# The inverse 47-point step of a spectral layer with FFN: segments of 8 n1, cosine and sine rows in one product, one copy out

## The chip, the cores and the metric

The kernel runs on one core of a Trainium2 chip. The metric is the device time of one execution in microseconds, the median of several runs; the trace comes from one further execution that was profiled.

## The reference

```python
X = np.fft.rfft(x, axis=1)                      # x: 8 x 3008 x 256
Yr = Xr @ w_r - Xi @ w_i + b_r                  # D = 256 mixed at each frequency
Yi = Xr @ w_i + Xi @ w_r + b_i
Y = shrunk(Yr) + 1j * shrunk(Yi)                # sign(a) * max(|a| - 0.01, 0)
y = np.fft.irfft(Y, n=3008, axis=1)
...
h = y @ w_in                                    # 24064 tokens x 2048
g = h * np.clip(h + 3, 0, 6) / 6
out = g @ w_out                                 # 24064 x 256
```

## The kernel before

The transform over 3008 = 64 x 47 positions is done in two steps with matrices, over n1 (64) and n2 (47). Since the input is real, 24 of the 47 frequencies k2 suffice. For each of 8 batches `stage1` makes the 47-point transforms of the input and stores them in DRAM (`scr1`), `middle` does the 64-point transforms, the mixing with `w_r` and `w_i` and the shrinking, and the 64-point transforms back, and stores the result in DRAM (`scr2`: cosine or sine part, n1, k2, D). `segment(b, k)` does the last step, the sum over k2 for each n2, and writes y into `raw`, transposed: 128 partitions hold half of D (`dh` is the half), and the free axis holds positions, cut in chunks of T = 512 (`raw[c]`, two buffers).

A segment of before takes 10 n1 (the seventh of a batch takes 4). Its data `qt` comes with two loads, one for the cosine part and one for the sine part, each with 5 n1 x 24 k2 = 120 rows in 2 groups. For each half of D four products (cosine and sine, two groups; L847) give the even part and the odd part for 24 n2 each, 240 columns a part. ScalarE copies the odd part out of PSUM into `odd` (L857). VectorE adds both for n2 = 0 to 23 (`direct`, L862) and subtracts them for the mirrored n2 (`mirrored`, L876), into `raw`, cut where a chunk ends or where a run of 23 is broken. So the positions within a segment do not stand in natural order; the host puts them right at the end. The products are in full fp32, for which the trace shows two records, with a weight load each, for one matmul of the program.

`prepare(c)` takes `raw[c]` once it is whole: GpSimd forms four differences (L924), ScalarE rounds seven blocks (L130), and GpSimd makes the remainders (L131); the results are `yb`. The FFN runs over 47 chunks x 8 = 376 units (c, f). A unit multiplies `yb` by blocks of `w_in` in a Strassen scheme of seven products (`pb`, `ps_a`, all at L137); ScalarE copies the partial sums `p`, `u` and `h` (L946, L978), VectorE adds (L949), ScalarE applies the first part of the gate (`r`, L1001) and rounds (`gs`, L1006), VectorE does the rest (L1003, L1007), and the products with `w_out` add up in `po` (`down`).

The order is written out by hand. In the loop over units each unit has four places (`fill`), and `slots` says which step of which generator goes to which place: `begin[b, k]` is the unit in which a segment starts, at least 8.5 units ahead of the chunk in which it begins and 3 ahead of the next segment; `lay` spreads a segment's three steps (load, first half of D, second half) over three units. The first two segments of batch 0 and the third are laid by themselves, at the start. All loads and stores are issued on SyncE's queue, in program order. `ps_a` has four PSUM buffers, `qt` one, `raw` two.

Of the kernel before, what the change touches and what calls it, by code (L numbers as in the profile page):

```python
# [9 lines left out]
F32 = mybir.dt.float32  # L10
# [4 lines left out]
ALU = mybir.AluOpType  # L15
# [6 lines left out]
B, S, D, FF = 8, 3008, 256, 2048  # L22
N1, N2 = 64, 47
NK = N2 // 2 + 1
LAM = 0.01
P = 128

J = 5
SEGS = tuple((n1, min(2 * J, N1 - n1)) for n1 in range(0, N1, 2 * J))
R47 = J * NK  # L30
NFT = FF // P

T = 512
# [4 lines left out]
def sequence():  # L38

    n1, n2 = np.meshgrid(np.arange(N1), np.arange(N2), indexing="ij")  # L40
    return (N2 * n1 + N1 * n2) % S


def positions():

    pos, order = sequence(), []
    for first, n in SEGS:
        n1 = first + np.arange(n)
        order += [pos[n1, :NK].reshape(-1), pos[n1][:, N2 - np.arange(1, NK)].reshape(-1)]
    return np.concatenate(order)  # L50


def constants():

    n1, n2 = np.arange(N1), np.arange(N2)
    k1, k2 = np.arange(N1), np.arange(NK)
    freq = np.zeros((N1, NK), np.int64)
    for k in range(S):
        if k % N2 < NK:
            freq[k % N1, k % N2] = k  # L60
    sign = np.where(freq <= S // 2, 1.0, -1.0)
    t47 = 2 * np.pi * np.outer(k2, k2) / N2
    t64 = 2 * np.pi * np.outer(n1, k1) / N1
    c47, s47, c64, s64 = np.cos(t47), np.sin(t47), np.cos(t64), np.sin(t64)


    f47 = np.zeros((J, NK, 2, J, NK))
    for j in range(J):
        f47[j, :, 0, j] = c47
        f47[j, :, 1, j] = s47  # L70

    f64 = np.zeros((2, N1, NK, 2, N1))
    f64[0, :, :, 0] = c64[:, None]
    f64[1, :, :, 0] = -s64[:, None]
    f64[0, :, :, 1] = -s64[:, None] * sign.T[None]
    f64[1, :, :, 1] = -c64[:, None] * sign.T[None]

    g64 = np.zeros((2, N1, 2, N1))
    g64[0, :, 0] = c64.T
    g64[1, :, 0] = -s64.T  # L80
    g64[0, :, 1] = -s64.T
    g64[1, :, 1] = -c64.T
    g64 *= 2.0 / S

    sgn = np.ones((2, N1, 2, NK // 2))
    sgn[:, :, 1] = sign.reshape(N1, NK // 2, 2).transpose(2, 0, 1)
    sgn[0, N1 // 2 + 1 :, :, 0] = 0.0
    for k in (0, N1 // 2):
        sgn[0, k, 0, 0] = 0.5
        sgn[0, k, 1, 0] = 0.0  # L90
    f = lambda a, *s: np.ascontiguousarray(a.reshape(*s).astype(np.float32))
    return {
        "f47": f(f47, R47, 2 * R47),
        "f64": f(f64, P, NK * P),
        "g64": f(g64, P, P),
        "g64u": f(np.broadcast_to(g64.transpose(1, 0, 2, 3)[None], (2, N1, 2, 2, N1)), P, 2 * P),
        "sgn": f(sgn, P, NK),
    }


@with_exitstack
def spectral_ffn(ctx: ExitStack, tc: tile.TileContext, x, w_r, w_i, bias, w_in, w_out, f47, f64, g64, g64u, sgn, out):
    nc = tc.nc
    const = ctx.enter_context(tc.tile_pool(name="const", bufs=1))
    sb = ctx.enter_context(tc.tile_pool(name="sb", bufs=1))
# [8 lines left out]
    def space(shape, dt, name, tag=None):  # L114
        tag = tag or name
        return sb.tile(shape, dt, name=name, tag=tag, bufs=depth.get(tag, 1))
# [187 lines left out]

    f47_s = [const.tile([R47, 2 * R47], dt, name="f47_" + t) for t, dt in (("hi", F32R), ("lo", F32R), ("all", F32))]
    nc.sync.dma_start(out=f47_s[2], in_=f47)
    scr1, scr2 = {}, {}

    def rows_of(b, n1, w):
# [389 lines left out]
    band()  # L699
    band()  # L700
    nc.sync.dma_start(out=g64u_s, in_=g64u)
    nc.sync.dma_start(out=bias_s[P // 2 :], in_=bias[P // 2 :])
    warm(8)
    split(*w_re)
# [112 lines left out]
    raw = {}  # L817

    def segment(b, k):
        n1, n = SEGS[k]  # L820
        gr = 2 if n == 2 * J else 1
        rows = n // gr * NK
        w = n * NK
        t0 = b * S + n1 * N2
        begins = b == 0 and k < 2
        qt = space([P, 2, 2, D], F32, "qt", "r" if begins else "xin" if (b, k) == (0, 2) else "qt")
        for cs in range(2):
            src = scr2[b][cs, n1 : n1 + n].rearrange("(g j) k d -> (j k) g d", g=gr)
            nc.sync.dma_start(out=qt[:rows, cs, :gr], in_=src)
        for c in range(t0 // T, (t0 + n * N2 - 1) // T + 1):  # L830
            if c not in raw:
                raw[c] = space([P, 2, T], F32, "raw")
        yield

        def places(at, size):

            done = 0
            while done < size:
                c, q = divmod(t0 + at + done, T)
                m = min(size - done, T - q)  # L840
                yield c, q, at + done, at + done + m
                done += m

        def products(ps, dh, groups):
            for cs in range(2):
                for g in groups:
                    nc.tensor.matmul(  # L847
                        out=ps[:, cs * w + g * rows : cs * w + (g + 1) * rows],
                        lhsT=qt[:rows, cs, g, dh * P : (dh + 1) * P],
                        rhs=f47_s[2][:rows, cs * R47 : cs * R47 + rows],  # L850
                        start=True,
                        stop=True,
                    )

        def odd_part(ps, n):
            odd = space([P, 2 * R47], F32, "odd", "p1" if begins else "xi")[:, :n]
            nc.scalar.copy(out=odd, in_=ps[:, w : w + n])  # L857
            return odd

        def direct(ps, odd, dh, lo, hi):  # L860
            for c, q, lo, hi in places(lo, hi - lo):
                nc.vector.tensor_tensor(out=raw[c][:, dh, q : q + hi - lo], in0=ps[:, lo:hi], in1=odd[:, lo:hi], op=ALU.add)  # L862

        def mirrored(ps, odd, dh):
            some = lambda a: a.rearrange("p (n q) -> p n q", q=NK)[:, :, 1:]
            m = NK - 1
            for c, q, lo, hi in places(w, n * m):
                lo, hi = lo - w, hi - w
                while lo < hi:
                    row, col = divmod(lo, m)  # L870
                    if col == 0 and hi - lo >= m:
                        r1, c1 = hi // m, m
                    else:
                        r1, c1 = row + 1, min(m, col + hi - lo)
                    size = (r1 - row) * (c1 - col)
                    nc.vector.tensor_tensor(  # L876
                        out=raw[c][:, dh, q : q + size].rearrange("p (n q) -> p n q", n=r1 - row),
                        in0=some(ps[:, :w])[:, row:r1, col:c1],
                        in1=some(odd)[:, row:r1, col:c1],
                        op=ALU.subtract,  # L880
                    )
                    lo, q = lo + size, q + size

        if (b, k) == (0, 1):
            lead = T - t0
            pss = [room(), room()]
            for dh in range(2):
                products(pss[dh], dh, range(1))
            for dh in range(2):
                direct(pss[dh], odd_part(pss[dh], lead), dh, 0, lead)  # L890
            yield
            for dh in range(2):
                products(pss[dh], dh, range(1, gr))
                odd = odd_part(pss[dh], w)
                direct(pss[dh], odd, dh, lead, w)
                mirrored(pss[dh], odd, dh)
                yield
            return
        for dh in range(2):
            ps = room()  # L900
            products(ps, dh, range(gr))
            odd = odd_part(ps, w)
            direct(ps, odd, dh, 0, w)
            mirrored(ps, odd, dh)
            yield


# [198 lines left out]
    per = S / 64  # L1106
    begin = {}
    for b in reversed(range(B)):
        for k in reversed(range(len(SEGS))):
            first = 8 * ((b * S + SEGS[k][0] * N2) // T)  # L1110
            begin[b, k] = min([first - 8.5, *([begin[b, k + 1] - 3] if (b, k + 1) in begin else [])])
            if k + 1 == len(SEGS) and (b + 1, 0) in begin:
                begin[b, k] = min(begin[b, k], begin[b + 1, 0] - 3)
    for c in range(1, NC):
        g = prepare(c)
# [9 lines left out]
        slots.setdefault(q, []).append(g)  # L1125
    lay(g, 15, 7.5, 12.5)
    for b in range(B):
        for k in range(len(SEGS)):
            if (b, k) not in ((0, 0), (0, 1)):
                if (b, k) == (0, 2):  # L1130
                    lay(segment(b, k), 3, 1, 2.5)
                else:
                    lay(segment(b, k), 3, max(0, begin[b, k]), max(3, begin[b, k] + 3))
        if b:
            pairs(middle(b), max(13, per * (b - 1) - 14), begin[b, 0] - 1.5)
        if b > 1:
            lay(stage1(b), 16, max(14, per * (b - 2) - 10), per * (b - 1) - 16)
# [93 lines left out]
```

## Time and profile before

| | |
|---|---|
| median of 3 runs | 2578.67 us (2576.99 to 2579.1) |
| the profiled execution | 2579.09 us |
| its span, first to last instruction | 2577.3 us |
| granted TensorE clock | 1.000 of full speed |

Of the profiled execution's time all but 1.8 us lies in the span. An engine's share of busy time is over the whole span; "x" is a count of instructions. Matmuls overlap and their ends are modelled, so the distance from one start to a later one tells more than a duration. In groups of instructions, the numbers behind the bar are the busy time in us and the mean of one instruction in ns, and behind the second bar the idle time of the engine ahead of them and what ended it. Of the stages: up to 98 us the first transforms run; from 98 us the FFN's units run, the first of them beside what is left of the weights' preparation; from 140 us on they run steadily, and the transforms of the next batches are laid between them.

### The profile page before, as it was taken

The numbers are of one execution on the slowest core, as the hardware profiler recorded it, in microseconds if no ns is written. First come the engines' busy times: TensorE is split into PE (matmuls) and PEld (weight loads), VectorE is DVE, ScalarE is ACT, GpSimd is POOL, SyncE is SP. The second block draws the span as 40 slices with busy tenths as digits, with TensorE's granted clock in tenths as the row PEclk, the third lists the DMA queues.
The fourth block names the chain that finished last, engine by engine and source line by source line (L and its number), as shares of the span: only waits on it lengthen the run. The fifth ranks groups of instructions, "written<-read, shape, count | busy, mean of one in ns | idle before, by whom it ended". The sixth has DMA issues, their size and how long they took to land.

```text
span 2577.3 us, 45562 instructions
## 1 busy us (share of the span) xinstructions
PE 2558.3 (99%) x16502; PEld 2290.4 (89%) x16502; DVE 1952.9 (76%) x3169; ACT 1965.1 (76%) x4330; POOL 741.5 (29%) x722
## 2 busy tenths in 40 slices
PE   9999999999999999999999999999999999999999
PEld 6788889899999989988899888999999999999998
DVE  6978877777777877777777777777777777766676
ACT  5777777777777777777777777777777777777877
POOL 2233422343133421433313432133411221121210
PEclk9999999999999999999999999999999999999999
DMA  8534422232122221222212322222321121110000
GB/s 279 173 93 133 131 73 69 83 95 73 57 79 82 88 83 49 83 83 80 81 55 77 91 87 67 64 77 84 91 62 53 56 73 49 37 32 25 20 17 17
DMA packets 147209, 199.65 MB, mean 77 GB/s; under 512 B 16303, under 2 KB 101927, under 8 KB 146983
## 3 DMA queue, kind: packets, MB, share of 16 engines
q1 hardware_dynamic: 146983, 196.73, 25.2%
q8 instruction: 130, 2.13, 0.3%
q14 instruction: 96, 0.79, 0.1%
HBM read 99.68 MB, written 74.97 MB: 68 GB/s over the span
## 4 chain that ended last, share of the span: by engine, by line
PE 90%; DVE 4%; ACT 3%; DMA 2%; issue 1%; POOL 0%; SPq 0%; DVEq 0%; ACTq 0%; POOLq 0%
PE po L137 38%; PE ps_a L137 25%; PE pb L137 19%; PE ps_a L847 3%; PE ps_a L737 3%; PE ps_a L459 1%; DVE r L1003 1%; DVE gs L1007 1%; ACT gs L1006 1%; DVE h L949 1%; DMA xin<-in_x 0%; ACT r L1001 0%; PE ps_a L494 0%; PE pb L426 0%; DMA scr<-a 0%
## 5 line engine op out<-in xcount | busy, mean ns | idle before, releaser
L137 PE MATMUL po<-gs,w_out_hi 128*128 128x512 f32 x3008 | 948.4, 396 | 1.5 <-DVE gs L1007 1.4
L1001 ACT ACTIVATE r<-h,three 128x512 f32<-128x512 f32 x750 | 541.7, 725 | 149.7 <-DVE h L949 135.1
L1003 DVE SCALAR_TENSOR_TENSOR r<-r,h 128x1024 f32<-128x1024 f32 x375 | 491.1, 1309 | 212.0 <-ACT r L1001 210.9
L137 PEld LDWEIGHTS po<-gs,w_out_hi 128*128 128x128 f32 x3008 | 565.1, 188 | 87.4 <-DVE gs L1007 3.9
L137 PE MATMUL po<-gs,w_out_lo 128*128 128x512 f32 x1504 | 611.3, 406 | 0.2 <-ACT gs L1006 0.2
L1007 DVE TENSOR_TENSOR gs<-r,gs 128x1024 fp32r<-128x1024 f32 x375 | 479.4, 1278 | 163.9 <-ACT gs L1006 163.4
L137 PE MATMUL pb<-yb,w_in_hi 128*128 128x256 f32 x3008 | 564.6, 280 | 0.0
L1006 ACT CAST gs<-r 128x512 fp32r<-128x512 f32 x750 | 429.1, 620 | 175.1 <-DVE r L1003 172.0
L137 PEld LDWEIGHTS pb<-yb,w_in_hi 128*128 128x128 f32 x3008 | 460.9, 188 | 33.3
L131 POOL TENSOR_TENSOR yb<-T,yb 128x256 fp32r<-128x256 f32 x184 | 193.0, 1051 | 840.2 <-ACT yb L130 840.1
L137 PE MATMUL ps_a<-yb,w_in_hi 128*128 128x256 f32 x2256 | 432.6, 280 | 0.1
L137 PE MATMUL pb<-yb,w_in_lo 128*128 128x256 f32 x1504 | 423.7, 282 | 3.9 <-ACT p L946 2.0
L949 DVE TENSOR_TENSOR h<-ps_a,u 128x256 f32<-128x256 f32 x752 | 313.8, 417 | 133.2 <-PE ps_a L137 129.7
L137 PEld LDWEIGHTS ps_a<-yb,w_in_hi 128*128 128x128 f32 x2256 | 345.4, 188 | 17.2 <-DVE yb L131 0.3
L946 ACT COPY u<-pb 128x256 f32<-128x256 f32 x752 | 279.3, 372 | 104.1 <-PE pb L137 102.4
L137 PE MATMUL ps_a<-yb,w_in_lo 128*128 128x256 f32 x1128 | 318.2, 282 | 3.0 <-DVE h L949 2.5
L137 PEld LDWEIGHTS pb<-yb,w_in_lo 128*128 128x128 f32 x1504 | 283.3, 188 | 42.0 <-ACT p L946 3.5
L137 PEld LDWEIGHTS po<-gs,w_out_lo 128*128 128x128 f32 x1504 | 283.5, 188 | 20.4 <-issue 2.4
L137 PEld LDWEIGHTS ps_a<-yb,w_in_lo 128*128 128x128 f32 x1128 | 212.0, 188 | 25.6 <-DVE h L949 8.6
L946 ACT COPY p<-pb 128x256 f32<-128x256 f32 x376 | 138.7, 369 | 38.2 <-PE pb L137 36.4
L949 DVE TENSOR_TENSOR h<-ps_a,p 128x256 f32<-128x256 f32 x376 | 156.4, 416 | 3.2 <-ACT p L946 2.6
L131 POOL TENSOR_TENSOR xs<-xin,xs 120x512 fp32r<-120x512 f32 (+1 forms) x42 | 55.2, 1314 | 310.7 <-ACT xs L130 288.5
(165 smaller groups left out, 3456.1 us busy)
## 6 DMA issues: line engine op xcount, KB each, us to landing
xin<-in_x SPq DMA_DIRECT2D x48, 512.0 KB, 3.6
bt<-scr SPq DMA_DIRECT2D x96, 256.0 KB, 3.1
scr<-pt SPq DMA_DIRECT2D x96, 256.0 KB, 2.0
out<-ot SPq DMA_DIRECT2D x93, 256.0 KB, 2.0
scr<-a SPq DMA_DIRECT2D x96, 240.0 KB, 2.5
qt<-scr SPq DMA_DIRECT2D x96, 240.0 KB, 3.5
zt<-tc SPq DMA_DIRECT2D x336, 64.0 KB, 2.0
f<-in_f SPq DMA_DIRECT2D x96, 128.0 KB, 2.8
```

The costliest lines, as they stand in the source:

```text
L131: (on or nc.vector).tensor_tensor(out=lo, in0=src, in1=hi.bitcast(F32), op=ALU.subtract)
L137: nc.tensor.matmul(out=ps, lhsT=a, rhs=b, start=start and n == 0, stop=stop and n == len(todo) - 1, skip_group_check=more,)
L459: nc.tensor.matmul(out=to, lhsT=x[:, xh, dh, which], rhs=w_s[w][wh][:, dh * D : (dh + 1) * D], start=False, stop=n == 2 and (which, dh) == ...
L737: nc.tensor.matmul(out=psv[:, dh, :, u, :], lhsT=data[:, u, dh * P : (dh + 1) * P], rhs=f[:, u, :], start=True, stop=True,)
L847: nc.tensor.matmul(out=ps[:, cs * w + g * rows : cs * w + (g + 1) * rows], lhsT=qt[:rows, cs, g, dh * P : (dh + 1) * P], rhs=f47_s[2][:row ...
L946: nc.scalar.copy(out=t, in_=ps)
L949: nc.vector.tensor_tensor(out=hs[i][:, u, half * H : (half + 1) * H], in0=ps, in1=keep.pop((i, n)), op=ALU.add)
L1001: nc.scalar.activation(out=r[:, u], in_=h[:, u], func=AF.Relu, bias=three, scale=1.0)
L1003: nc.vector.scalar_tensor_tensor(out=r, in0=r, scalar=6.0, in1=h, op0=ALU.min, op1=ALU.mult)
L1006: nc.scalar.copy(out=t[:, 0, u], in_=r[:, u])
L1007: nc.vector.tensor_tensor(out=t[:, 1], in0=r, in1=t[:, 0].bitcast(F32), op=ALU.subtract)
```

## The change

A segment takes 8 n1, eight to a batch. `qt` now has 96 rows (2 n1 x 24 k2 of cosine, and below them as many of sine) in 4 groups of two n1. A new constant `i47` of 96 rows and 2 x 47 = 94 columns holds cosine and sine for all 47 n2, so that one product gives two n1 in full, in natural order. For each half of D there are four products of 96 rows and 94 columns, beside each other in one PSUM tile of 376 columns. One copy per half moves the result into `raw`, cut where a chunk ends: ScalarE moves the first half of D, VectorE the second. `odd`, `direct`, `mirrored` and `places` go. The slots are laid for eight segments. `positions` becomes natural order.

```diff
+PARTS = tuple(range(0, N1, 8))
...
+    turn = 2 * np.pi * np.outer(k2, n2) / N2
+    i47 = np.zeros((2, 2, NK, 2, N2))
+    for j in range(2):
+        i47[0, j, :, j] = np.cos(turn)
+        i47[1, j, :, j] = np.sin(turn)
...
+    i47_s = const.tile([4 * NK, 2 * N2], F32, name="i47")
...
     nc.sync.dma_start(out=g64u_s, in_=g64u)
+    nc.sync.dma_start(out=i47_s, in_=i47)
     nc.sync.dma_start(out=bias_s[P // 2 :], in_=bias[P // 2 :])
...
     def segment(b, k):
-        n1, n = SEGS[k]
-        gr = 2 if n == 2 * J else 1
-        rows = n // gr * NK
-        w = n * NK
-        t0 = b * S + n1 * N2
+        n1, w = PARTS[k], 2 * N2
+        rows = 2 * NK
+        t0, size = b * S + n1 * N2, 4 * w
...
-        qt = space([P, 2, 2, D], F32, "qt", "r" if begins else "xin" if (b, k) == (0, 2) else "qt")
+        qt = space([P, 4, D], F32, "qt", "r" if begins else "xin" if (b, k) == (0, 2) else "qt")
         for cs in range(2):
-            src = scr2[b][cs, n1 : n1 + n].rearrange("(g j) k d -> (j k) g d", g=gr)
-            nc.sync.dma_start(out=qt[:rows, cs, :gr], in_=src)
+            src = scr2[b][cs, n1 : n1 + 8].rearrange("(g j) k d -> (j k) g d", g=4)
+            nc.sync.dma_start(out=qt[cs * rows : (cs + 1) * rows], in_=src)
...
         def products(ps, dh, groups):
-            for cs in range(2):
-                for g in groups:
-                    nc.tensor.matmul(
-                        out=ps[:, cs * w + g * rows : cs * w + (g + 1) * rows],
-                        lhsT=qt[:rows, cs, g, dh * P : (dh + 1) * P],
-                        rhs=f47_s[2][:rows, cs * R47 : cs * R47 + rows],
-                        start=True,
-                        stop=True,
-                    )
...
+            for g in groups:
+                nc.tensor.matmul(
+                    out=ps[:, g * w : (g + 1) * w],
+                    lhsT=qt[: 2 * rows, g, dh * P : (dh + 1) * P],
+                    rhs=i47_s,
+                    start=True,
+                    stop=True,
+                )
+
+        def moved(ps, dh, lo, hi):
+            while lo < hi:
+                c, q = divmod(t0 + lo, T)
+                m = min(hi - lo, T - q)
+                to, of = raw[c][:, dh, q : q + m], ps[:, lo : lo + m]
+                if dh:
+                    nc.vector.tensor_copy(out=to, in_=of)
+                else:
+                    nc.scalar.copy(out=to, in_=of)
+                lo += m
...
         for dh in range(2):
             ps = room()
-            products(ps, dh, range(gr))
-            odd = odd_part(ps, w)
-            direct(ps, odd, dh, 0, w)
-            mirrored(ps, odd, dh)
+            products(ps, dh, range(4))
+            moved(ps, dh, 0, size)
             yield
...
-        for k in reversed(range(len(SEGS))):
-            first = 8 * ((b * S + SEGS[k][0] * N2) // T)
+        for k in reversed(range(len(PARTS))):
+            first = 8 * ((b * S + PARTS[k] * N2) // T)
```

## Rows read from the trace of the kernel before

**Rows 1.** The page: busy time of each engine, its share of the span and its instructions.

```profile
PE 2558.3 (99%) x16502; PEld 2290.4 (89%) x16502; DVE 1952.9 (76%) x3169; ACT 1965.1 (76%) x4330; POOL 741.5 (29%) x722
```

**Rows 2.** Busy time by stage, four windows from the start of the span. Columns: the window in us and its length, then for TensorE matmul, TensorE weight load, VectorE, ScalarE and GpSimd the busy us and (x) the instructions, then the granted TensorE clock, the DMA share and GB/s.

```profile
98.00:140.00 42.00, 36.67 (x231) 31.37 (x232) 40.18 (x83) 31.37 (x76) 10.76 (x10) 1.00 0.46 142
140.00:1000.00 860.00, 855.87 (x5541) 770.16 (x5540) 657.41 (x1049) 658.79 (x1468) 285.62 (x265) 1.00 0.29 85
1000.00:2000.00 1000.00, 997.81 (x6493) 902.81 (x6492) 767.47 (x1247) 765.60 (x1702) 306.18 (x284) 1.00 0.25 75
2000.00:2490.00 490.00, 490.00 (x3180) 444.55 (x3179) 357.02 (x580) 381.62 (x828) 103.05 (x117) 1.00 0.13 40
```

**Rows 3.** The page: the chain of work that ended last, share of the span by engine.

```profile
PE 90%; DVE 4%; ACT 3%; DMA 2%; issue 1%; POOL 0%; SPq 0%; DVEq 0%; ACTq 0%; POOLq 0%
```

**Rows 4.** Groups of instructions by line and form, whole span.

```profile
L847 PE MATMUL ps_a<-f_all,qt 120*128 120x120 f32 x768 | 101.5, 274 | 1.5 <-ACT a L397 0.8 <-DMA qt<-scr 0.7
L847 PEld LDWEIGHTS ps_a<-f_all,qt 120*128 120x128 f32 x768 | 100.2, 191 | 10.3 <-ACT a L397 1.6 <-DMA qt<-scr 1.0 <-DVE raw L862 0.3
...
L847 PEld LDWEIGHTS ps_a<-f_all,qt 96*128 96x128 f32 x64 | 9.6, 191 | 1.3
...
L847 PE MATMUL ps_a<-f_all,qt 96*128 96x96 f32 x64 | 9.3, 267 | 0.0
...
L599 PE MATMUL ps_a<-e,f_all 120*120 120x512 f32 x8 | 4.1, 591 | 0.0
```

**Rows 5.** TensorE matmuls in order of time around a segment of 10 n1: start in us, time in us, line, tiles, form, count of merged records.

```profile
1097.04 1.05 PE L847 MATMUL ps_a<-f_all,qt 120*128 120x120 f32 x8
1097.85 0.48 PE L137 MATMUL po<-gs,w_out_lo 128*128 128x512 f32 x1
1098.16 0.62 PE L137 MATMUL po<-gs,w_out_hi 128*128 128x512 f32 x2
1098.62 0.28 PE L137 MATMUL pb<-yb,w_in_lo 128*128 128x256 f32 x1
```

**Rows 6.** The same around a segment of 4 n1.

```profile
1299.62 0.58 PE L847 MATMUL ps_a<-f_all,qt 96*128 96x96 f32 x4
...
1300.30 0.62 PE L137 MATMUL po<-gs,w_out_hi 128*128 128x512 f32 x2
```

**Rows 7.** The same at two fp32 products of 512 columns.

```profile
151.14 1.02 PE L599 MATMUL ps_a<-e,f_all 120*120 120x512 f32 x2
```

**Rows 8.** Busy time of single lines in the windows 98 to 140 and 140 to 2577 us, columns as in rows 2 but of the line's engine alone: the two lines of VectorE's L862, the two of its L876, the first of TensorE's L847.

```profile
98.00:140.00 42.00, 2.87 (x10) 1.00 0.46 142
140.00:2577.00 2437.00, 43.06 (x148) 1.00 0.23 69
...
98.00:140.00 42.00, 2.32 (x6) 1.00 0.46 142
140.00:2577.00 2437.00, 46.94 (x230) 1.00 0.23 69
...
98.00:140.00 42.00, 7.10 (x48) 1.00 0.46 142
```

**Rows 9.** Groups by line and form: VectorE's and ScalarE's copies out of PSUM, and the eviction of a full segment.

```profile
L357 DVE COPY a<-pb 120x512 f32<-120x512 f32 x5 | 3.5, 692 | 2.6 <-PE pb L346 1.9 <-ACT a L359 0.7
...
L506 DVE COPY pt<-po 128x256 f32<-128x256 f32 x1 | 0.4, 424 | 0.3 <-PE po L494 0.3
...
L946 ACT COPY u<-pb 128x256 f32<-128x256 f32 x752 | 279.3, 372 | 104.1 <-PE pb L137 102.4
...
L580 ACT COPY a<-ps_a 120x512 f32<-120x512 f32 x80 | 46.2, 577 | 3.7 <-PE ps_a L137 2.6 <-DMA scr<-a 0.8
...
L857 ACT COPY odd<-ps_a 128x240 f32<-128x240 f32 x96 | 34.4, 358 | 24.6 <-PE ps_a L847 18.1 <-DVE X L131 5.5 <-DVE raw L876 0.2
...
L862 DVE TENSOR_TENSOR raw<-ps_a,odd 128x240 f32<-128x240 f32 x52 | 20.9, 401 | 0.8
```

**Rows 10.** Who waited for whom from 140 us on, TensorE's weight loads: us in total, times, longest.

```profile
PEld ps_a L137 <- DVE h L949: 9.0, 17, 1.0
...
PEld ps_a L737 <- DMA bt<-scr: 0.2, 1, 0.2
```

**Rows 11.** GpSimd, ScalarE and VectorE in order of time at one hand-over of `raw`.

```profile
2111.48 0.73 POOL L131 TENSOR_TENSOR yb<-raw,yb 128x256 fp32r<-128x256 f32 x1
...
2112.19 0.36 ACT L857 COPY odd<-ps_a 128x240 f32<-128x240 f32 x1
...
2113.46 0.47 DVE L862 TENSOR_TENSOR raw<-ps_a,odd 128x40 f32<-128x40 f32 x2
```

**Rows 12.** The same at another.

```profile
1851.33 1.77 POOL L131 TENSOR_TENSOR yb<-raw,yb 128x256 fp32r<-128x256 f32 x1
...
1851.41 0.36 ACT L857 COPY odd<-ps_a 128x240 f32<-128x240 f32 x1
...
1853.13 0.39 DVE L862 TENSOR_TENSOR raw<-ps_a,odd 128x222 f32<-128x222 f32 x1 [0.21 <-POOL yb L131]
```

**Rows 13.** The page, DMA issues: count, KB each, median us from issue to landing.

```profile
qt<-scr SPq DMA_DIRECT2D x96, 240.0 KB, 3.5
```

**Rows 14.** SyncE's issues in order of time.

```profile
26.31 0.47 SPq L702 DMA_DIRECT2D bias<-in_bias  x1
28.15 0.33 SPq L415 DMA_DIRECT2D f<-in_f  x1
```

More of the change, by code (lines that the diff above doesn't have):

```diff
@@ L44, in positions @@
 def positions():
[L46 to L50, printed above, removed]
+    return sequence().reshape(-1)
 def constants():
@@ L93, in constants @@
         "f47": f(f47, R47, 2 * R47),
+        "i47": f(i47, 4 * NK, 2 * N2),
         "f64": f(f64, P, NK * P),
@@ L101, in spectral_ffn @@
 @with_exitstack
-def spectral_ffn(ctx: ExitStack, tc: tile.TileContext, x, w_r, w_i, bias, w_in, w_out, f47, f64, g64, g64u, sgn, out):
+def spectral_ffn(ctx: ExitStack, tc: tile.TileContext, x, w_r, w_i, bias, w_in, w_out, f47, i47, f64, g64, g64u, sgn, out):
     nc = tc.nc
@@ L819, in segment @@
     def segment(b, k):
-        n1, n = SEGS[k]
-        gr = 2 if n == 2 * J else 1
-        rows = n // gr * NK
-        w = n * NK
-        t0 = b * S + n1 * N2
+        n1, w = PARTS[k], 2 * N2
+        rows = 2 * NK
+        t0, size = b * S + n1 * N2, 4 * w
         begins = b == 0 and k < 2
-        qt = space([P, 2, 2, D], F32, "qt", "r" if begins else "xin" if (b, k) == (0, 2) else "qt")
+        qt = space([P, 4, D], F32, "qt", "r" if begins else "xin" if (b, k) == (0, 2) else "qt")
         for cs in range(2):
-            src = scr2[b][cs, n1 : n1 + n].rearrange("(g j) k d -> (j k) g d", g=gr)
-            nc.sync.dma_start(out=qt[:rows, cs, :gr], in_=src)
-        for c in range(t0 // T, (t0 + n * N2 - 1) // T + 1):
+            src = scr2[b][cs, n1 : n1 + 8].rearrange("(g j) k d -> (j k) g d", g=4)
+            nc.sync.dma_start(out=qt[cs * rows : (cs + 1) * rows], in_=src)
+        for c in range(t0 // T, (t0 + size - 1) // T + 1):
             if c not in raw:
@@ L833, in segment @@
         yield
[L835 to L842, printed above, removed]
-        def products(ps, dh, groups):
-            for cs in range(2):
-                for g in groups:
-                    nc.tensor.matmul(
-                        out=ps[:, cs * w + g * rows : cs * w + (g + 1) * rows],
-                        lhsT=qt[:rows, cs, g, dh * P : (dh + 1) * P],
-                        rhs=f47_s[2][:rows, cs * R47 : cs * R47 + rows],
-                        start=True,
-                        stop=True,
-                    )
@@ L855, in odd_part @@
[L855 to L882, printed above, removed]
@@ L887, in segment @@
             for dh in range(2):
-                products(pss[dh], dh, range(1))
-            for dh in range(2):
-                direct(pss[dh], odd_part(pss[dh], lead), dh, 0, lead)
+                products(pss[dh], dh, range(2))
+                moved(pss[dh], dh, 0, lead)
             yield
             for dh in range(2):
[L893 to L896, printed above, removed]
+                products(pss[dh], dh, range(2, 4))
+                moved(pss[dh], dh, lead, size)
                 yield
@@ L1108, in spectral_ffn @@
     for b in reversed(range(B)):
-        for k in reversed(range(len(SEGS))):
-            first = 8 * ((b * S + SEGS[k][0] * N2) // T)
+        for k in reversed(range(len(PARTS))):
+            first = 8 * ((b * S + PARTS[k] * N2) // T)
             begin[b, k] = min([first - 8.5, *([begin[b, k + 1] - 3] if (b, k + 1) in begin else [])])
-            if k + 1 == len(SEGS) and (b + 1, 0) in begin:
+            if k + 1 == len(PARTS) and (b + 1, 0) in begin:
                 begin[b, k] = min(begin[b, k], begin[b + 1, 0] - 3)
@@ L1127, in spectral_ffn @@
     for b in range(B):
-        for k in range(len(SEGS)):
+        for k in range(len(PARTS)):
             if (b, k) not in ((0, 0), (0, 1)):
```

## The prediction

> **What bounds the kernel now.** I read the table of the engines first: TensorE's matmul row is busy 99% of the span, VectorE 76% [rows 1]. A busy matmul row alone does not prove a bound, so the second view was the same by stage. From 140 to 2490 us no window has TensorE more than half a per cent idle, while VectorE and ScalarE have over a fifth of the time free; from 98 to 140 us it is the other way round: VectorE is busy 40.18 of 42.00 us and TensorE idle for 5.3 us [rows 2]. The granted clock is 1.00 in all of them, the level of 2.4 GHz, so it plays no part. The chain of waits says the same: 90% TensorE [rows 3]. So a microsecond of TensorE's stream costs a microsecond nearly everywhere, and a microsecond of VectorE counts only between 98 and 140 us.
>
> The third view is that of the products that the change rewrites, L847. One matmul of the program is two records in the trace (two weight loads, two matmuls): 832 records, 768 with 120 columns and 64 with 96 [rows 4]. The records' own durations (274 and 267 ns) are of no use, because neighbours overlap. What counts is how far a group pushes back the matmuls behind it, and this is read in the order of time. With 120 columns, eight records start at 1097.04, and the second output matmul behind them at 1098.16. An output matmul takes 0.23 us by itself (two of them from 1098.16 to 1098.62), and one stands between. So the group cost 1.12 - 0.23 = 0.89 us, 111 ns a record [rows 5]. With 96 columns and 96 rows, four records: 1300.30 - 1299.62 - 0.23 = 0.45 us, 112 ns a record [rows 6]. A fifth fewer columns and a fifth fewer rows cost the same. In both a weight load of 128 columns goes ahead of each matmul record (96x128 in the weight loads' row of the smaller form [rows 4]). So this product is paid by the record, through its weight load, and not by its columns. Where there are many columns, these set the price: two records of 512 columns last 1.02 us together [rows 7] against 0.59 for one [rows 4], a step of 0.43 us or 0.84 ns a column. By that slope 94 columns would need 79 ns, which is under 112.
>
> **The change, part by part.** *Products.* Before, a batch has six segments of 10 n1 (2 halves of D x 4 products) and one of 4 (2 x 2): 52 products, 104 records, times 8 batches 832, as the trace has. After, a batch has eight segments of 8 n1, each 2 x 4 products: 64 products, 128 records, 1,024 in all. The columns fall (6,144 to 6,016 a batch), the records rise by 192. The first three segments of batch 0, which lie before 140 us, have 48 records before [rows 8] and 48 after, so all 192 lie behind 140 us, where TensorE is the bound. At 112 ns: +21.5 us. Bounds: at 79 ns for all 1,024 it would be 80.9 - 93.2 = -12.3 us; above 112 no row of this shape goes. I take 112, because 94 columns by 96 rows is all but the group of 96 by 96.
>
> That a load of fewer rows costs no less is also what the Trainium skill says (TensorE: Matmul & The Clock Gate, "LDWEIGHTS (loading the stationary operand)"), and it speaks against this change: a load costs its columns over 1.2 GHz, whatever the rows, 106.7 ns for 128. By it the sum would be 192 x 106.7 ns = 20.5 us in place of 21.5; the trace agrees within 5 ns a record.
>
> *Eviction.* Removed: a ScalarE copy of the odd half (358 ns for 240 columns) and VectorE's adds and subtractions, 401 ns for a full direct half [rows 9] and about as much for the mirrored one, cut again at each chunk of 512 positions. Behind 140 us these are 43.06 + 46.94 us of VectorE [rows 8]; ScalarE's copies are 34.4 us for the full segments [rows 9]. Added: a copy of 376 columns, the first half of D on ScalarE, the second on VectorE. ScalarE copies take 372 ns for 256 columns and 577 for 512, so 468 for 376; VectorE's 424 and 692, so 550 [rows 9]. Some 61 segments x 0.55 us and 45 cuts at about 0.16 (where that slope meets no columns at all) make 41 us of VectorE, down by some 49; ScalarE stays near its 35.
>
> Between 98 and 140 us the old adds hold 2.87 + 2.32 = 5.2 us of a full VectorE [rows 8]. The new copies there have 376, 136, 240 and 376 columns (the last cut at position 1,024): 0.55 + 0.30 + 0.41 + 0.44 + 0.27 = 2.0 us. Relief 3.2 us; TensorE can give back no more than the 5.3 us it idles. Bounds 0 and -5.3; I take -3, near VectorE's saving, because VectorE is the full engine there.
>
> Behind 140 us TensorE's idle time is 4.1 + 2.2 + 0.0 = 6.3 us up to 2490 [rows 2], so relief gives between 0 and -6.3. Weight loads waited 9.0 us behind VectorE's add L949, in 17 places [rows 10]; a VectorE with 2% less to do will miss a few of them. I take -1.5.
>
> *A new wait: ScalarE behind GpSimd.* `raw` has two buffers: chunk c+2 is written into the buffer from which GpSimd still reads chunk c. Today all such writes are VectorE's, and they come late, behind ScalarE's `odd` copy. At 2111 us GpSimd's last read ends at 2112.21; ScalarE's copy started at 2112.19 and VectorE's write only at 2113.46, 1.25 us to spare [rows 11]. At 1851 us that read ends at 1853.10, ScalarE's copy had started at 1851.41, and VectorE's write stood until 1853.13 [rows 12]. After the change ScalarE itself writes `raw`, so it arrives about where `odd` starts now, and stands. Queued behind it on ScalarE are the copies `u`, `p` and `h`, which release TensorE's accumulators, and the gate's `r` and `gs`. There are 45 such hand-overs. At 2111 it would not wait; at 1851 for a microsecond or so. Bounds: 0 if TensorE has work enough queued, and rival C below. I take +1.5, which cancels the relief.
>
> *Loads.* `qt` has 16 loads a batch for 14, of 192 KB for 240 [rows 13]; both must have landed before the first product, where today the first starts products on its own. They are issued a unit of the program (2577.3 / 376 = 6.9 us) ahead of the products and land in 3.5 us [rows 13], and TensorE waited for them 0.7 us in all [rows 4]. `qt` has one buffer, so each load also holds SyncE's queue, with `zt`, `pt`, `xin` and `out` behind it, until the segment before it has been read; but of all DMAs, weight loads behind 140 us waited for one, `bt`, 0.2 us [rows 10]. Nothing. The table `i47` is one more issue on SyncE, some 0.47 us like its neighbour `bias`, at 26.8 us, where SyncE issues nothing until 28.15 [rows 14]; without that cover it would cost 0.5. Natural order of positions and the slots for eight segments issue no further instruction.
>
> **Sum.** The profiled execution took 2579.1 us; + 21.5 - 3 - 1.5 + 1.5 = 2597.6. The median of the runs is 0.4 us lower than that execution, so I say 2597.
>
> **Rivals.** (A) *The products go by columns*, faster than before: with fewer rows the load hides, and 94 columns cost 79 ns: 2579.1 - 12.3 - 3 = 2564. It turns the sign where a record costs under 94 ns (1,024 x 94 ns = 96.2 us, against 93.2 + 3). For it: long rows go by the column [rows 7]. Against it: 96 columns would then cost 81 ns and cost 112 [rows 6]. Chance 0.06. [...] (B) *The relief is full*: all of 5.3 + 6.3 us of idle time comes back: 2579.1 + 21.5 - 11.6 = 2589. For it: VectorE is what the weight loads wait for most [rows 10]; against it: every stall would have to hang on the segments' eviction. Chance 0.12. (C) *ScalarE's waits at the hand-overs pass on*: 45 x about 0.9 us (between none and the 1.7 us of [rows 12]), a third of it reaching TensorE: +13.5, so 2611 with the other terms as they are. For it: ScalarE's place at 1851 us [rows 12]; against it: the buffer was just free at 2111 us [rows 11]. Chance 0.13. (D) *The change does not do what it says*: the pieces at chunk cuts multiply and VectorE keeps its load. Then the 3 us are lost: 2600.6, inside the main case.
>
> **Numbers.** The main case has 0.69, with its own range 2592 to 2603. The range from 2587 to 2609 takes in B and the near part of C; it leaves out A and the rest of C. Faster by over 0.2% (5 us, about what a measurement of this kernel can tell): A, 0.06. Within 0.2%: 0.03, for B with some weight loads hidden besides. Slower: 0.91.
>
> **What would show it.** L847's rows: 1,024 records of 96 rows by 94 columns, eight of them pushing the next matmuls back by 0.90 us; 0.63 would be rival A. VectorE's busy share down by about 2 points, TensorE's unchanged. TensorE's idle time between 98 and 140 us down by some 3 us. Among ScalarE's waits a new line, `raw` behind GpSimd's `yb`; if TensorE then waits longer for `p`, `u` or `h`, it is rival C. The prediction is wrong if the record's price falls with the columns, or if those waits pass on.

## The result and the profile after

The changed kernel takes 2598.24 us, the median of six runs (2595.4 to 2598.54), against 2579.23 us of six runs before. The ratio is 1.0072 with a 95% interval of 1.0062 to 1.0082: slower by 19.0 us. The forecast was 2597 us, slower with 0.91. The number was right; the terms behind it were only partly so, and most of this part is about that.

The page of the kernel after, whose span is 2596.3 us in an execution of 2598.11: busy time of each engine, then the chain of work that ended last.

```profile
PE 2572.7 (99%) x16694; PEld 2307.0 (89%) x16694; DVE 1910.5 (74%) x2885; ACT 1965.3 (76%) x4326; POOL 780.7 (30%) x722
...
PE 90%; DVE 3%; ACT 2%; issue 2%; DMA 1%; POOL 1%; SPq 0%; DVEq 0%; ACTq 0%
```

TensorE has 192 records more and is as full as before, and VectorE lost two points, 42 us [rows 1, 3]. That so large a relief did not outweigh 192 records is the first thing to see: the engine that was relieved bounded next to nothing. GpSimd, which has the same 722 instructions, is busy 39 us longer (741.5 before [rows 1], 780.7 after). Nearly all of it lies in the four differences that it forms out of `raw`: its two groups went from 811 and 830 ns an instruction to 1048 and 996. Why is open; with segments of 8 n1 and the old eviction, a run below, they stayed at 835 and 813.

Groups of the kernel after by line and form: the products, and the two copies of a half that no chunk end cuts (18 of 64 on each engine).

```profile
L841 PEld LDWEIGHTS ps_a<-i,qt 96*128 96x128 f32 x1024 | 133.8, 191 | 12.5 <-ACT a L402 1.9 <-issue 0.2
L841 PE MATMUL ps_a<-i,qt 96*128 96x94 f32 x1024 | 131.7, 271 | 1.1 <-DMA qt<-scr 1.1
...
L855 DVE COPY raw<-ps_a 128x376 f32<-128x376 f32 x18 | 9.8, 543 | 3.2 <-PE ps_a L841 3.0
L857 ACT COPY raw<-ps_a 128x376 f32<-128x376 f32 x18 | 8.6, 475 | 5.2 <-PE ps_a L841 4.9
```

The record count and the two copies (543 and 475 ns, forecast 550 and 468) are as worked out. TensorE's matmuls around one group of the kernel after, in order of time (start, time, line, tiles, form, merged records):

```profile
1223.44 1.03 PE L841 MATMUL ps_a<-i,qt 96*128 96x94 f32 x8
1224.25 0.48 PE L141 MATMUL po<-gs,w_out_lo 128*128 128x512 f32 x1
1224.57 0.63 PE L141 MATMUL po<-gs,w_out_hi 128*128 128x512 f32 x2
```

Read as in [rows 5]: 1224.57 - 1223.44 - 0.23 = 0.90 us for eight records, 112 ns each, what 120 columns cost too. Busy time by stage of the kernel after, columns as in [rows 2]:

```profile
98.00:140.00 42.00, 37.59 (x245) 32.60 (x244) 39.26 (x76) 32.15 (x75) 11.60 (x9) 1.00 0.46 141
140.00:1000.00 860.00, 852.54 (x5546) 767.26 (x5545) 641.42 (x956) 651.08 (x1453) 295.16 (x261) 1.00 0.28 85
1000.00:2000.00 1000.00, 996.74 (x6536) 904.17 (x6535) 742.25 (x1110) 761.96 (x1693) 318.90 (x286) 1.00 0.25 75
2000.00:2490.00 490.00, 489.33 (x3188) 443.97 (x3187) 345.82 (x520) 377.62 (x814) 110.00 (x110) 1.00 0.13 40
```

From 140 to 2490 us TensorE now idles 7.5 + 3.3 + 0.7 = 11.4 us, where it idled 6.3 before [rows 2]. VectorE is freer and TensorE waits more. The waits from 140 us on say where (us in total, times, longest):

```profile
PEld ps_a L141 <- DVE h L920: 13.1, 19, 1.5
...
ACT raw L857 <- POOL yb L135: 12.0, 8, 4.0
...
PE ps_a L141 <- DVE h L920: 6.2, 12, 1.1
...
PEld pb L141 <- ACT h L949: 1.7, 1, 1.7
...
PE pb L141 <- ACT h L949: 1.3, 1, 1.3
```

The first line answers to [rows 10], where it had 9.0 us in 17 places. The matmuls behind the same add, and the weight load behind ScalarE's `h`, had less before:

```profile
PE ps_a L137 <- DVE h L949: 2.9, 9, 0.7
...
PEld pb L137 <- ACT h L978: 0.2, 1, 0.2
```

VectorE's add reads `u` and `p`, which ScalarE makes, so a late ScalarE can show in the add's line too. The line of ScalarE's `raw` is the new wait that the prediction named. The longest of its eight, in order of time on GpSimd, ScalarE and TensorE:

```profile
458.17 1.72 POOL L135 TENSOR_TENSOR yb<-T,yb 128x256 fp32r<-128x256 f32 x1
459.85 1.30 POOL L627 TENSOR_TENSOR xin<-xin 120x512 f32<-120x512 f32 x1
461.11 0.72 POOL L135 TENSOR_TENSOR yb<-raw,yb 128x256 fp32r<-128x256 f32 x1
...
457.42 0.44 ACT L857 COPY raw<-ps_a 128x336 f32<-128x336 f32 x1
461.86 0.19 ACT L857 COPY raw<-ps_a 128x40 f32<-128x40 f32 x1 [4.00 <-POOL yb L135]
461.95 0.38 ACT L917 COPY u<-pb 128x256 f32<-128x256 f32 x1
462.22 0.39 ACT L949 COPY h<-pb 128x256 f32<-128x256 f32 x1
...
462.66 0.39 PE L141 MATMUL pb<-yb,w_in_lo 128*128 128x256 f32 x1 [1.31 <-ACT h L949]
```

The segment crosses into a chunk whose buffer GpSimd still reads, because a transform's `xin` at 459.85 came between two of its remainders. ScalarE's last 40 columns stand for 4.00 us, `u` and `h` stand behind them, and TensorE stands for 1.31 us at 462.66, for a copy that takes 0.19.

### The profile page after: what moved, and what is told of

Same layout as the page of the kernel before. It is cut to its first block, busy times and chain, and to the rows that moved or that the text cites. A ratio compares the mean times of both kernels' runs of the same rounds, so it can differ in the third digit from the quotient of the medians.

```text
span 2596.3 us, 45651 instructions
## 1 busy us (share of the span) xinstructions
PE 2572.7 (99%) x16694; PEld 2307.0 (89%) x16694; DVE 1910.5 (74%) x2885; ACT 1965.3 (76%) x4326; POOL 780.7 (30%) x722
## 4 chain that ended last, share of the span: by engine, by line
PE 90%; DVE 3%; ACT 2%; issue 2%; DMA 1%; POOL 1%; SPq 0%; DVEq 0%; ACTq 0%
PE po L141 38%; PE ps_a L141 24%; PE pb L141 19%; PE ps_a L841 4%; PE ps_a L743 3%; PE ps_a L464 1%; DMA xin<-in_x 1%; DVE h L920 0%; DVE gs L978 0%; PE ps_a L499 0%; PE pb L431 0%; ACT r L972 0%; PE ps_a L604 0%; DVE r L974 0%; ACT gs L977 0%
```

## The experiments

**Records alone.** In the kernel before, one of the four products of a half is cut in two at 60 columns in full segments: 192 records more, no other work.

```diff
-                    nc.tensor.matmul(
+                    cut = rows // 2 if (cs, g) == (1, 1) else rows
+                    for lo in range(0, rows, cut):
+                        nc.tensor.matmul(
...
```

> The kernel before, with one of the four products of each half of D in a full segment (sine part, second group) cut in two at column 60: the same columns, the same evictions and slots, 96 matmuls and so 192 records more. Theory (a record costs its weight load, 112 ns): 192 x 0.112 = +21.5 us, of which 12 records lie before 140 us and may be hidden, so 2599 to 2601 us. Rival (the product is paid by columns): no change, 2579. Rival (the loss of the change comes from its eviction or its slots): no change here either, 2579.

Measured 2598.99 us against 2578.97, ratio 1.0076 (1.0061 to 1.0091): +20.0 us, or 104 ns a record. Its matmuls around a group, now ten records:

```profile
1102.79 1.22 PE L849 MATMUL ps_a<-f_all,qt 120*128 120x120 f32 x10
1103.82 0.48 PE L137 MATMUL po<-gs,w_out_lo 128*128 128x512 f32 x1
1104.14 0.63 PE L137 MATMUL po<-gs,w_out_hi 128*128 128x512 f32 x2
```

1104.14 - 1102.79 - 0.23 = 1.12 us, 0.23 more than the eight of [rows 5] with not a column more. The number of records alone costs about what the whole change cost; the interval is some 4 us either way.

**Segments of 8 n1 with the old products** (four of 96 by 96 a half, even and odd part) and the old eviction:

```diff
+PARTS = tuple((n1, 8) for n1 in range(0, N1, 8))
...
-        n1, n = SEGS[k]
-        gr = 2 if n == 2 * J else 1
+        n1, n = PARTS[k]
+        gr = 2
...
```

> The kernel before with eight segments of 8 n1 a batch, but its own products (cosine and sine apart, 4 n1 to a group: 96 rows by 96 columns) and its own eviction through odd, direct and mirrored: 1,024 records as after the change, eight segments in the slots, the eviction of before. Theory (records): +21.5 us and nothing back from the eviction, 2599 to 2603 us, so 1 to 4 us slower than the changed kernel. Rival (the loss sits in the one copy and ScalarE's waits behind GpSimd): 2579 to 2583.

Measured 2602.71 us, ratio 1.0088 (1.0071 to 1.0105). So the loss comes with the segments of 8 n1 already under the old products and the old eviction. It is 23.7 us, 3.7 more than for the records alone, which is within the two intervals.

**Columns.** `i47` padded with columns of zeros, to 128, 160 and 208 (W stands for the number in the code); the columns too many are overwritten or never read.

```diff
+        "i47": f(np.pad(i47.reshape(4 * NK, 2 * N2), ((0, 0), (0, W - 2 * N2))), 4 * NK, W),
...
-                    out=ps[:, g * w : (g + 1) * w],
+                    out=ps[:, g * w : g * w + W],
```

> The changed kernel with 128 columns in every product: i47 has 34 more columns of zeros, which the next product of the tile overwrites, or which nobody reads. Theory (a record costs its weight load up to 112 / 0.84 = 133 columns): no change from the changed kernel, 2596 to 2600 us, start to start 112 ns. Rival (columns, 0.84 ns each): 34 x 0.84 = 29 ns more on each of 1,024 records, +29 us, 2627.

> The changed kernel with 160 columns in every product, 66 of them zeros that are overwritten or not read. Theory (the larger of weight load, 112 ns, and columns at 0.84 ns): 134 ns a record, 976 records where TensorE is the bound x 22 ns = +21.9 us on the changed kernel, 2618 to 2622. Rival (columns alone): 66 x 0.84 = 55 ns more a record, +57 us, 2655. Rival (a record has a fixed price whatever its columns): 2598.

> The changed kernel with 208 columns in every product, 114 of them zeros that are overwritten or not read; one more point of the price by columns. Theory (the larger of 112 ns and 0.84 ns a column): 175 ns a record, 976 x 63 ns = +61 us on the changed kernel, 2657 to 2661. Rival (columns come on top of the weight load): 112 + 114 x 0.84 = 208 ns, +93 us, 2691.

Measured 2602.82 us (ratio 1.0092, 1.0077 to 1.0107), 2619.39 (1.0156, 1.0140 to 1.0171) and 2660.99 (1.0315, 1.0296 to 1.0334). The group with 128, 160 and 208 columns, a fence for each:

```profile
1225.13 1.05 PE L841 MATMUL ps_a<-i,qt 96*128 96x128 f32 x8
...
1226.25 0.62 PE L141 MATMUL po<-gs,w_out_hi 128*128 128x512 f32 x2
```

```profile
1227.09 1.25 PE L841 MATMUL ps_a<-i,qt 96*128 96x160 f32 x8
...
1228.42 0.62 PE L141 MATMUL po<-gs,w_out_hi 128*128 128x512 f32 x2
```

```profile
1243.03 1.57 PE L841 MATMUL ps_a<-i,qt 96*128 96x208 f32 x8
...
1244.67 0.63 PE L141 MATMUL po<-gs,w_out_hi 128*128 128x512 f32 x2
```

Less 0.23 us and over eight: 111, 138 and 176 ns a record. The first is the price of 94 columns, the last two are 0.86 and 0.85 ns a column, close to the slope of [rows 7]. So the price is the larger of 112 ns and some 0.85 ns a column; from these two numbers the corner is estimated near 132 columns, and the runs place it between 128 and 160. With 160 and 208 columns the times came out as expected. But with 128 columns the kernel was 4.6 us slower than with 94, while its groups were not: the theory's 2596 to 2600 was missed, and the groups could not be the reason.

**The copies on other engines.** VectorE moves the first half of D and ScalarE the second (first diff), or VectorE moves both (second).

```diff
-                if dh:
+                if not dh:
                     nc.vector.tensor_copy(out=to, in_=of)
```

```diff
-                if dh:
-                    nc.vector.tensor_copy(out=to, in_=of)
-                else:
-                    nc.scalar.copy(out=to, in_=of)
+                nc.vector.tensor_copy(out=to, in_=of)
```

> The changed kernel with the two copies exchanged: VectorE moves the first half of D, ScalarE the second, a unit later. Theory (ScalarE's waits behind GpSimd, 12.0 us in 8 places in the changed kernel, hardly reach TensorE): those waits go to under 2 us, the time stays within 2 us of the changed kernel, 2596 to 2600. Rival (these waits pass on to TensorE): 5 to 12 us faster than the changed kernel, 2586 to 2593.

> The changed kernel with both copies on VectorE, as the adds of before were: VectorE has some 35 us more to do, ScalarE 35 us less and no wait behind GpSimd. Theory (behind 140 us the engines beside TensorE hardly count; from 98 to 140 us VectorE is the bound): 1 to 4 us slower than the changed kernel, most of it by the unit that starts near 154 us, 2599 to 2602. Rival (ScalarE's waits at the hand-overs cost time): faster than the changed kernel, 2588 to 2595.

The swap took 2592.71 us (ratio 1.0045, 1.0031 to 1.0059), 5.5 less than the changed kernel, as the rival had it and not the theory. With the two halves swapped ScalarE comes to the buffer second, and its line "raw behind yb" is gone; VectorE has it, and TensorE's two lines behind VectorE's add fell from 13.1 and 6.2 us:

```profile
PEld ps_a L141 <- DVE h L920: 10.0, 21, 1.5
...
DVE raw L855 <- POOL yb L135: 5.4, 6, 2.3
...
PE ps_a L141 <- DVE h L920: 1.6, 3, 1.1
```

Busy time by stage of the swap, from 140 us on:

```profile
140.00:1000.00 860.00, 855.96 (x5566) 770.29 (x5565) 642.76 (x960) 654.44 (x1457) 290.27 (x262) 1.00 0.28 85
1000.00:2000.00 1000.00, 998.76 (x6545) 905.40 (x6545) 743.92 (x1112) 765.70 (x1698) 315.00 (x285) 1.00 0.25 75
2000.00:2490.00 490.00, 489.87 (x3193) 444.54 (x3193) 345.65 (x518) 379.32 (x817) 105.30 (x111) 1.00 0.12 39
```

TensorE idles 4.0 + 1.2 + 0.1 = 5.4 us there, 6.0 less than the 11.4 of the changed kernel, and the time fell by 5.5. So ScalarE's standing at the hand-overs cost about 6 us. Three other kernels of this section with ScalarE's wait (128 columns, 160 columns, and W = 34 below; 10.8 to 13.4 us of it) idle 9.4 to 12.8 us in the same windows; with 208 columns the wait is 8.9 us and TensorE idles 6.4. With both copies on VectorE TensorE idles 7.2 us, and the time was 2595.06 us, ratio 1.0061 (1.0048 to 1.0074): 3.2 less than after, where 2599 to 2602 was expected. VectorE has room for both.

**The first three segments alone.** Those of batch 0 the new way, all others as before. Batch 0 then has a full segment where before had its short one, so there are 8 records more (840):

```diff
+PARTS = {0: tuple((n1, 8) for n1 in (0, 8, 16)) + tuple((n1, 10) for n1 in (24, 34, 44, 54))}
+PARTS.update({b: SEGS for b in range(1, B)})
...
```

> The first three segments of batch 0 as in the change (8 n1, one copy), all others as before (10 n1, even and odd part; batch 0 has four of them, 8 records more than before). Theory (the eviction's gain sits between 98 and 140 us, some 2.5 us, and the loss in the records): +0.9 - 2.5 = -1.6 us against before, 2577 to 2579, and TensorE's units run 2 us or more ahead of those of before, counted from the first product of a segment. Rival (the gain is spread over the whole run): 2580.

Measured 2574.46 us over 11 runs, ratio 0.9982 (0.9973 to 0.9991): faster than both kernels, and by more than these segments were expected to give (2577 to 2579). The trace showed no stall that had gone; the units, also those near the end, were about 11 ns shorter. Like the changed kernel, this one holds `i47`, 94 columns of 4 bytes (376 bytes of each partition) that stand among the constants, and all tiles allocated behind them stand that much further on. That gave the theory of the next runs: the distance itself changes the matmuls' steps.

**Distance alone.** An unused constant of W columns, zeroed once, is added behind the others; nothing uses it.

```diff
+    pad = const.tile([P, W], F32, name="pad")
+    nc.gpsimd.memset(pad, 0.0)
     scr1, scr2 = {}, {}
```

> The kernel before with one unused constant of 94 columns (376 bytes a partition, cleared once by GpSimd), where the changed kernel and e7 allocate i47: every tile allocated behind it lies 376 bytes higher in SBUF, and nothing else differs. Theory (the uniform 11 to 12 ns a unit that the changed kernel, e5, e6 and e7 are ahead, without a stall, come from where the tiles lie): 376 units x 11.5 ns = -4.3 us, 2574 to 2576, and the step between two matmuls of pb and ps_a falls as in e7 (from the last block's end to the next block's start 119.4 to 117.0 ns). Rival (they come from less eviction work): 2579, steps as before.

> The kernel before with an unused constant of 64 columns (256 bytes): one more place for the tiles behind it. Theory (placement counts, and not the presence of a constant): a time of its own between 2572 and 2582, with steps that differ from those of before or of e9. Rival (any shift does what 376 bytes do): as e9.

> The changed kernel with an unused constant of 34 columns (136 bytes), so that i47 and it take 512 bytes as the i47 of 128 columns in e3 did. Theory (placement): the steps of before and of e3, +4 us on the changed kernel, 2601 to 2604, although no product has a column more. Rival (e3's +4.6 us is the price of 34 columns more a product): 2596 to 2600.

> The kernel before with an unused constant of 8 columns (32 bytes of each partition) behind the others, so that all tiles allocated after the constants lie 32 bytes further on; no work on TensorE, VectorE or ScalarE changes. Theory of placement, with the distance taken modulo 256 bytes: before's tiles then stand as those of after with 160 bytes did (384 + 160 = 544, which is 32 modulo 256), the run in which the step from one half of pb to its next was 114.2 ns in place of 116.5 and the time fell by 9.6 us against after, which stood at 128 modulo 256 and was itself some 4.5 us better off than before by e9. So 2579.5 - 4.5 - 9.6 = about 2565 us, range 2562 to 2570, with steps of about 114 ns. Rival: the 9.6 us of that run came from something of the changed kernel's own tiles (its four tiles of 752 bytes and i47), and the kernel before moved by 32 bytes gains nothing or only what e9 showed: 2574 to 2581 us, steps of 116 to 119 ns.

Distances are of what stands behind the constants, against the kernel before. They are reckoned with each tile rounded up to a multiple of 32 bytes (376 to 384, 136 to 160); no trace shows addresses, so this is a premise. The last column is the distance from the first to the last segment product, from which differences of the start have dropped out.

| kernel | bytes further | modulo 256 | median us | ratio (95%) | first to last product |
|---|---|---|---|---|---|
| before | 0 | 0 | 2579.23 | | 2389.2 |
| before, W = 64 | 256 | 0 | 2579.92 | 1.0002 (0.9993 to 1.0011) | 2389.9 |
| before, W = 94 | 384 | 128 | 2574.71 | 0.9981 (0.9972 to 0.9990) | 2384.3 |
| before, W = 8 | 32 | 32 | 2566.09 | 0.9947 (0.9933 to 0.9960) | 2375.0 |
| after with 128 columns | 512 | 0 | 2602.82 | 1.0092 (1.0077 to 1.0107) | 2410.7 |
| after | 384 | 128 | 2598.24 | 1.0072 (1.0062 to 1.0082) | 2406.7 |
| after, W = 34 | 544 | 32 | 2588.62 | 1.0035 (1.0021 to 1.0049) | 2398.3 |

An unused constant of 32 bytes a partition makes the kernel before 0.5% faster, which beats every other kernel here. The products of its segments, then its last steady stage, columns as in [rows 2]; and for comparison the products of the kernel before:

```profile
L849 PE MATMUL ps_a<-f_all,qt x832: 246/275/370, 97.5 to 2472.5; 120*128 120x120 f32 x154, 96*128 96x96 f32 x13
```

```profile
2000.00:2490.00 490.00, 490.00 (x3205) 445.21 (x3204) 360.04 (x579) 382.11 (x832) 103.91 (x115) 1.00 0.13 39
```

```profile
L847 PE MATMUL ps_a<-f_all,qt x832: 247/275/370, 98.3 to 2487.5; 120*128 120x120 f32 x154, 96*128 96x96 f32 x13
```

The same 832 records, the last of them 15.0 us earlier; and in a window in which TensorE never idles in either kernel, 3,205 records in place of the 3,180 of [rows 2]. No wait was removed (from 140 to 2490 us TensorE idles 7.6 us with W = 8, against 6.3): the steps are shorter. Worked out from the starts of the matmuls between 2000 and 2540 us, mean ns from one start to the next ("lo" and "hi" are the halves of the weights, in the order of the kernel):

| step | before | before, W = 94 | before, W = 8 | after | after, W = 34 |
|---|---|---|---|---|---|
| `pb` hi to `pb` hi | 116.5 | 117.5 | 113.8 | 117.6 | 114.2 |
| `pb` hi to `pb` lo | 119.4 | 117.0 | 114.0 | 117.6 | 115.1 |
| `pb` hi to `ps_a` lo | 118.3 | 115.8 | 114.1 | 115.9 | 114.3 |
| `po` hi to `po` hi | 233.2 | 232.3 | 232.8 | 232.4 | 232.9 |

The columns pair off by the distance modulo 256 (128: the second and fourth; 32: the third and fifth), not by which kernel it is, though not every step does. The other kernels fall in with them: in the first two rows the four more at 0 have 116.5 to 116.8 and 119.3 to 120.5 ns, the four more at 128 have 117.3 to 117.7 and 117.0 to 117.7. A fourth place is in the record too: with 208 columns, 832 bytes on, 64 modulo 256, these steps are 116.9 and 120.2, no better than at 0. Not any shift helps: 256 bytes did nothing. W = 8 was the run that could have ended the theory, and 2566.09 came against "about 2565". W = 34 in the changed kernel had been expected at 2601 to 2604, as slow as with 128 columns, because 376 + 136 bytes are 512, and came out 13 us under that. Two kernels at the same distance can't differ so by the theory; the rounding, which makes it 544, was reckoned with only from then on, and W = 8 was its test.

## Why the prediction was right, and where it was not

*The change by itself, at equal distance.* The table gives it three times: 2602.82 over before at 0, ratio 1.0092; at 128, 1.0072 / 0.9981 = 1.0091; at 32, 1.0035 / 0.9947 = 1.0088. So the change alone costs 0.9%, some 23 us, and about 4.9 of these were given back because `i47` happened to push the tiles to a better distance. Segments of 8 n1 with the old products and the old eviction, at distance 0, cost as much (1.0088): at equal distance the new products and copies together gave nothing back. The sum of the prediction was +18.5 us and the measured difference +19.0, but their terms are not the same:

| term | forecast | measured | by |
|---|---|---|---|
| 192 records | +21.5 | +20.0 | records alone |
| VectorE's relief, 98 to 140 us | -3 | about -1 | three segments against W = 94, both at 384 bytes: -0.3, with 8 records more (0.9) |
| relief behind 140 us | -1.5 | about -1 | idle time of the swap, 5.4, against 6.3 |
| ScalarE behind GpSimd | +1.5 | about +6 | idle time of after, 11.4, against the swap's 5.4 |
| distance of the tiles | not seen | -4.9 | W = 94 against before |
| sum | +18.5 | about +19 | |

*The records* were the step that carried the forecast, and it was right in size: the price of a record does not fall with its columns below some 130, so rival A had no ground. That it is the weight load that sets the 112 ns is not shown: all these products load 128 weight columns, and no run loads fewer.

*The relief from 98 to 140 us* is a term that came out smaller than forecast. VectorE did lose busy time there, but only 0.9 us (40.18 to 39.26), and TensorE's idle time fell from 5.3 to 4.4 [rows 2], where some 3 had been forecast. The run with three segments gives about 1 us; its interval and that of W = 94 are some 2 us wide either way, so the -3 is not excluded by it alone. Part of what was lost is a later start. Last matmul of the first transforms and first product, before and then after:

```profile
96.55 1.02 PE L389 MATMUL pb<-e,f_all 120*120 120x512 f32 x2
98.33 0.68 PE L847 MATMUL ps_a<-f_all,qt 120*128 120x120 f32 x4 [0.76 <-ACT a L397]
99.29 1.82 PE L847 MATMUL ps_a<-f_all,qt 120*128 120x120 f32 x14 [0.28 <-DMA qt<-scr]
```

```profile
97.53 1.02 PE L394 MATMUL pb<-e,f_all 120*120 120x512 f32 x2
99.61 3.60 PE L841 MATMUL ps_a<-i,qt 96*128 96x94 f32 x28 [1.07 <-DMA qt<-scr]
```

The first product of the kernel after needs both loads, a step that the prediction put at nothing, and TensorE stands 1.07 us there; but before it stood 0.76 and 0.28 us at this place too. The first product is 1.28 us later, and 0.98 us of this is already there at the transforms' last matmul. In all eight kernels with the new products in the first segment it started between 98.9 and 100.5 us, in the six with the old ones between 96.9 and 98.3. Of the 2.0 us between their means, 0.8 are there before 15 us and 1.2 before 40 us, where no segment runs yet; why it fell so is not settled.

*The relief behind 140 us* was small, as said; the 0.9 us are less than one profile differs from the next. *The hand-overs* are the term that was mis-sized most, by 4.5 us. By the prediction's own sign ("if those waits pass on") it was wrong here. The mechanism was the one described, and it is rival C's: ScalarE stands, and `u`, `h` and the gate behind it. The two places that the prediction read [rows 11, 12] gave waits of nothing and about a microsecond; the eight real ones reach 4.0 us, where a transform's work lies between GpSimd's remainders. Of ScalarE's 12.0 us about half reached TensorE. C had 45 waits and 13.5 us: too many places, and each too small. (C's 2611 keeps the main case's 1.5 us beside the 13.5 that take their place; 2597.6 - 1.5 + 13.5 is 2609.6.)

*The distance* was missing from the list altogether. It has the opposite sign to the errors in the relief and the hand-overs and most of their size. That the time came out within 2 us of the forecast was luck; without the distance it would have been 2603, still inside the range given. Nor does the measured column's sum of 19 prove its terms: each is known to a microsecond or more, the records to some 4.

Rival B's 2589 came nearest in the swap, 2592.71, but for another reason: ScalarE no longer stands, while the idle time that B wanted back, 6.3 us behind 140, was still 5.4. Rival D fell with the copies' count: VectorE's instructions went from 3,169 to 2,885.

## What to carry to other kernels

Here a full-fp32 product of few columns was paid by the record (112 ns up to 128 columns), so count records, and fill columns up to the corner before cutting work into more products. A copy that is moved to an engine with releasing duties takes its buffer's wait with it; put it where it comes late, or on the engine that has room. And whenever an edit adds or resizes a tile, a difference of some tenths of a per cent may be the tiles' place: run the old kernel with an unused tile of the same size as a control before any other reason is given.

## What the runs showed of the hardware that was not expected

The steps of TensorE's matmuls depend on where the tiles behind the constants stand, by 1 to 5 ns of some 117 (table above), and the whole kernel by up to 13.5 us, 0.5%. The times of the seven kernels in the table fit the distance modulo 256 bytes with 32 best of 0, 32 and 128. Whether it is the weights, the moving data or the results that matter, and what in the memory does it, is open: only whole shifts were tried, and four places with the one at 64.

The second surprise is the granted clock near the start. In the swap and in the kernel with both copies on VectorE, the window from 104 to 108 us reads (first the swap, then the other; columns as in [rows 2]):

```profile
104.00:108.00 4.00, 4.00 (x22) 3.80 (x21) 3.24 (x11) 2.57 (x9) 0.00 (x0) 0.59 1.03 364
```

```profile
104.00:108.00 4.00, 3.92 (x18) 3.92 (x19) 1.74 (x6) 1.69 (x5) 0.00 (x0) 0.50 1.02 360
```

There the clock stands at its lower level, 1.2 GHz, for most or all of the stretch. A third kernel, with segments of 8 n1 and the old products, has it for about half of the same stretch:

```profile
104.00:108.00 4.00, 3.44 (x18) 2.96 (x18) 4.00 (x15) 3.64 (x12) 0.00 (x0) 0.74 0.88 308
```

TensorE had idled 1.7, 2.6 and 1.5 us of the six before it; but with 128 columns it had idled 1.7 us too, and the clock stayed at 1.00, so what decides is open. The first two profiled runs are therefore read from 140 us on alone, and the times of the swap spread more than others (2588.19 to 2594.8); whether by the clock is not shown.
